# First loads, unit sizes, casts and last group of an attention-then-MoE kernel rearranged on one Trainium2 core

## The chip, the cores and the metric

The kernel runs on 1 core of one Trainium2 (trn2) chip. The metric is device microseconds of one execution. Before the change the median of 4 runs is 959.17 us (958.56 to 964.36).

## The reference, cut to what matters

Attention with pooled keys feeds a two-layer MLP. All inputs and the output are float32.

```python
# B, C, Hh, Ww = 4, 128, 384, 32 ; r = 4 ; d_ff = 2048
kv_pool = kv.reshape(B, H//r, r, W//r, r, C).mean(axis=(2, 4))
kv_flat = kv_pool.reshape(B, -1, C) @ w_sr          # 768 keys per batch, k = v
s = scale * (q @ k.transpose(0, 2, 1))
a = np.exp(s - s.max(-1)); a /= a.sum(-1) + 1e-09
x = a @ v                                           # 49152 tokens x 128
h = x @ w_in                                        # 128 -> 2048
out = (h * (1 / (1 + np.exp(-1.702 * h)))) @ w_out  # 2048 -> 128
```

## The kernel before

**Tiling.** The 49152 tokens are cut into 96 groups of 512 (`NG`), four groups make a set (`s`, 24 of them), 24 groups are one batch. A batch has 768 keys in 6 chunks of 128 (`JC`). The MLP's 2048 hidden columns are 16 chunks of 128 (`FCH`). The work goes attention of groups 0 to 47, MLP of groups 0 to 47, attention of 48 to 95, MLP of 48 to 95. The attention of a few chunks (the four groups 48 to 51, and eight "rolling" chunks) has its exponential on VectorE instead of ScalarE.

**Units.** TensorE fills one half of PSUM banks 0 to 5 with up to three chunks of 128x512 scores (`fill_attn`, L335 to 340) or hidden values (`fill_moe`, L517 to 521); one ScalarE instruction evicts the unit as Exp or Gelu into `ag`. Units go alternately to banks 0 to 2 and 3 to 5, and unit p's fill waits for ScalarE's end of unit p-2. Later TensorE *drains* what was evicted: attention weights times V into bank 6 or 7 (`drain_attn`, L349), or w_out times the activations into bank 6 or 7 (`drain_moe`, L526). The list `sizes` (L542) gives the chunks of the first units: two of 1, seven of 2, then (3, 3, 2) four times; all others have 3. The first attention part has 286 chunks, so its last unit holds 1 chunk.

**Order.** The program is written out in order by hand. `first` (L600) names what TensorE does ahead of the first 21 units: pooling of key chunks (`pool_chunk`, L136), keys and values (L145, L150, L158, L159), transposes of q (`transpose_q`, L229) and dummy matmuls (`warm`, L286). `prepare` calls `background(i)` (L456) when group i is first met, and a loop with estimated costs (`COST`) places the drains and extras. Each engine runs its own instructions in this order.

**Loads.** At the start group 0 and group 1 of q come as float32 on SyncE's and ScalarE's queues into `ag` (L240), are cast by ScalarE (L258), transposed by TensorE (L229) and evicted by ScalarE (L233); groups 2 to 15 come by casting DMAs from GpSimd's queue (`load_q`, L218) and their transposes are evicted by VectorE (L235). The key chunks of batch 0 come in the same GpSimd queue (`load_chunk`, L127), the first two in halves. From set 4 on, q is cast in HBM to `q_bf` by GpSimd's queue (`cast_q`, L206) and loaded by a transposing DMA from SyncE's queue (`load_qT`, L211) into one of four `qT` buffers. In `background`, at every fourth group, set s+3 is loaded so and set s+5 is cast; `gate` (L447) is a one-element memset on VectorE followed by one on GpSimd over the same element, so that GpSimd's next DMA goes out only when VectorE has come to that place. At groups 10 and 13 three key chunks each of batch 1 are loaded.

**End.** A group's output gathers over 16 chunks as 128 output columns by 512 tokens in one bank, is transposed in 32x32 blocks by VectorE (L534) and leaves in four DMAs of 64 KB (L537), whose contiguous pieces are 32 floats, 128 bytes. For the last group two of them go by SyncE's queue and two by ScalarE's.

Of the kernel before, what the change touches and what calls it, by code (L numbers as in the profile page):

```python
# [7 lines left out]
F32 = mybir.dt.float32  # L8
F32R = mybir.dt.float32r
I32 = mybir.dt.int32  # L10
BF = mybir.dt.bfloat16
# [13 lines left out]
def kernel(  # L25
    ctx, tc, q, kv, w_sr, moe_w_in, moe_w_out, out,
):
    nc = tc.nc
# [7 lines left out]
    FCH = d_ff // 128  # L36
    scale = 1.0 / (C ** 0.5)
    G = 512
# [5 lines left out]
    K = 3  # L44
# [76 lines left out]
    def load_chunk(b, jc, n=1):  # L121

        a, ch = divmod(jc, HC)
        t = x_tile(XS - 1 - jc)
        for k in range(n):
            sl = slice(k * SG // n, (k + 1) * SG // n)
            nc.gpsimd.dma_start(out=t[:, sl], in_=kv_r[b, a, ch][:, sl])  # L127
        kv_tiles[b, jc] = t.rearrange("p (wp w1 c) -> p w1 wp c", w1=r, c=C)
# [75 lines left out]
    def cast_q(s):  # L204
        sl = slice(s * SG, (s + 1) * SG)
        nc.gpsimd.dma_start(out=q_bf[sl, :].rearrange("(p i) c -> p (i c)", p=128),  # L206
                            in_=q_flat[sl, :].rearrange("(p i) c -> p (i c)", p=128))

    def load_qT(s):
        qTs[s] = qpool.tile([128, 1, SG], BF, name="qT")  # L210
        nc.sync.dma_start_transpose(out=qTs[s], in_=q_bf[s * SG:(s + 1) * SG, :])  # L211


# [8 lines left out]
    def transpose_q(g):  # L222
        s = g // 4
        if g % 4 == 0:
            qTs[s] = qpool.tile([128, 1, SG], BF, name="qT")
        ps = acc_bf()[:, 0:G].rearrange("p (i t) -> p i t", i=4)
        for i in range(4):
            o = (g % 4) * G + i * 128
            nc.tensor.transpose(ps[:, i, :], qs[s][:, o:o + 128], ident)  # L229
        dst = qTs[s][:, 0, (g % 4) * G:(g % 4 + 1) * G].rearrange("p (t i) -> p t i", i=4)  # L230
        src = ps.rearrange("p i t -> p t i")
        if g < 2:
            nc.scalar.copy(dst, src)  # L233
        else:
            nc.vector.tensor_copy(dst, src)  # L235

    ag = agpool.tile([128, AG, 512], BF, name="ag")
    raw = ag[:, 0:4, :].bitcast(F32)
    for g, eng in ((0, nc.sync), (1, nc.scalar)):
        eng.dma_start(out=raw[:, 2 * g:2 * g + 2, :],  # L240
                      in_=q_flat[g * G:(g + 1) * G, :].rearrange("(p k i) c -> p k (i c)", p=128, k=2))
    w_sr_f = cpool.tile([128, C], F32)
    nc.sync.dma_start(out=w_sr_f, in_=w_sr)
    load_chunk(0, 0, 2)
    load_chunk(0, 1, 2)
    load_q(0, 2, 4)
    load_q(1, 0, 2)
# [6 lines left out]
    load_q(3, 0, 2)  # L254
    load_q(3, 2, 4)
    cast_q(4)
    for g in range(2):
        nc.scalar.copy(qs[0][:, g * G:(g + 1) * G].rearrange("p (k e) -> p k e", k=2), raw[:, 2 * g:2 * g + 2, :])  # L258

    ones = cpool.tile([128, 32], BF)  # L260
    nc.vector.memset(ones, 1.0)
# [21 lines left out]
    def warm(n):  # L283

        for _ in range(n):
            nc.tensor.matmul(banks[:32, 2, :], ones, ones.unsqueeze(1).broadcast_to([128, 16, 32]),  # L286
                             start=True, stop=True)
# [1 line left out]
    w_in_sb = cpool.tile([128, d_ff], BF)  # L289
    w_out_sb = cpool.tile([128, FCH, C], BF)  # L290

    warm(7)
    transpose_q(0)
    transpose_q(1)
    warm(4)


    slot_of = {}
# [148 lines left out]
    def gate():  # L447

        one = gate_tile[:, gates[0] % 8:gates[0] % 8 + 1]
        gates[0] += 1  # L450
        nc.vector.memset(one, 0.0)  # L451
        nc.gpsimd.memset(one, 0.0)  # L452

    CAST = 5

    def background(i):  # L456

        s = i // 4
        if i % 4 == 0:
            if QS <= s + 3 < NS:  # L460
                load_qT(s + 3)
            if CAST <= s + CAST < NS:
                gate()
                cast_q(s + CAST)
        if i in (10, 13):
            gate()
            for jc in range(i - 10, i - 7):
                load_chunk(1, jc)
        if 0 <= i - 16 < JC:
            extras.append((key_and_value, 1, i - 16))  # L470
        if 0 <= i - 15 < JC:
            extras.append((pool_chunk, 1, i - 15))
        if i in (30, 34, 38):
            put_away(0, (i - 30) // 4)
        if i in (33, 37, 41):
            bring_back(0, (i - 33) // 4)
        if i == 26:
            gate()
            nc.gpsimd.dma_start(out=w_in_sb, in_=moe_w_in)
        if i == 34:  # L480
            gate()
            nc.gpsimd.dma_start(out=w_out_sb, in_=moe_w_out.rearrange("(o p) c -> p o c", p=128))
# [40 lines left out]
    def drain_moe(g, fc):  # L523
        if fc == 0:
            o_of[g] = acc(("o", g))
        nc.tensor.matmul(o_of[g], w_out_sb[:, fc, :], weights(("m", g, fc)),  # L526
                         start=(fc == 0), stop=(fc == FCH - 1))
        del slot_of["m", g, fc]
        if fc == FCH - 1:
            close(("o", g), max(now, dve - 1.0) + EVACUATE)  # L530
            on_dve(3.6)

            o_sb = opool.tile([128, 512], F32, name="o_sb")
            nc.vector.transpose(o_sb, o_of.pop(g))  # L534
            for m in range(4):
                eng = nc.scalar if g == NG - 1 and m % 2 else nc.sync
                eng.dma_start(out=out_r[g, m],  # L537
                              in_=o_sb[32 * m:32 * m + 32, :].rearrange("i (b j) -> i b j", j=32))


    NA, NM = NG * JC, NG * FCH
    chunks, sizes = [], [1] * 2 + [2] * 7 + [3, 3, 2] * 4  # L542
    chunks += [(0, 0), (1, 0), (0, 1), (1, 1)]
    chunks += [(i, jc) for i in range(2, 8) for jc in range(2)]
    chunks += [(i, jc) for jc in range(2, JC) for i in range(8)]
# [3 lines left out]
    for n in range(R):  # L549
        part = [c for c in chunks if c[0] // (NG // R) == n]  # L550
        while part:
            m = sizes.pop(0) if sizes else K
            seq.append(("a", part[:m]))
            part = part[m:]
        todo += [("a", t, a) for t in range(n * NT // R, (n + 1) * NT // R) for a in range(2)
                 if (t // TS * TS + TS - 1) // 4 not in early]
        flat = [(g, fc) for g in range(n * NG // R, (n + 1) * NG // R) for fc in range(FCH)]
        todo += [("m",) + c for c in flat]
        for k in range(0, len(flat), K):
            seq.append(("m", flat[k:k + K]))  # L560

    at = {}
    for p, (kind, part) in enumerate(seq):
# [15 lines left out]
    def prepare(p):  # L579
# [18 lines left out]
                free[last_acc] = now + COST[f][1]  # L598

    first = {  # L600
        0: [(pool_chunk, 0, 0), (warm, 1), (key_chunk, 0, 0), (warm, 1)],
        2: [(value_chunk, 0, 0), (warm, 1), (pool_chunk, 0, 1), (warm, 1), (key_and_value, 0, 1), (warm, 1)],
        3: [(transpose_q, 2), (transpose_q, 3)],
        4: [(transpose_q, 4)],
        5: [(transpose_q, 5)],
        6: [(transpose_q, 6)],
# [141 lines left out]
```

## Time and profile before

| | |
|---|---|
| median of 4 runs | 959.17 us |
| the profiled execution, its time | 958.56 us |
| its span in the profile | 956.5 us |
| ScalarE (ACT) busy | 941.4 us, 98% |
| TensorE matmul (PE) busy | 942.7 us, 99% |
| VectorE (DVE) busy | 382.4 us, 40% |
| GpSimd (POOL) busy | 68.8 us, 7% |
| mean DMA rate | 99 GB/s |

The profile's page lists busy time by engine, the span in slices, the DMA queues, the chain of work that ended last, the costliest groups of instructions and the DMA issues. A matmul's duration in it overlaps that of the next one, so a busy PE is not a PE at its limit; the same is true of ScalarE, where an activation's record can begin while the one before still runs. The distance between the starts of two successive instructions is then the better measure. "L340" is line 340 of the kernel shown above. Times in the timeline are microseconds from the start of the span.

### The profile page before, as it was taken

How to read it: one execution, taken by the hardware profiler on the slowest of the kernel's cores; microseconds unless marked ns; L12 is line 12 of the kernel's file. 1: busy time of each engine (PE TensorE's matmuls, PEld its weight loads, DVE VectorE, ACT ScalarE, POOL GpSimd, SP SyncE). 2: the span in 40 equal slices, each digit the busy share in tenths (PEclk: the TensorE clock that was granted, in tenths of full speed). 3: DMA queues.
4: the chain of work that ended last, by engine and by line, in shares of the span. 5: the costliest groups of instructions: out<-in, count | busy, mean ns of one | idle time of the engine just before them, and what ended most of it. 6: DMA issues, size and time to landing. Idle time of an engine off the chain costs nothing.

```text
span 956.5 us, 15155 instructions
## 1 busy us (share of the span) xinstructions
PE 942.7 (99%) x6280; PEld 501.8 (52%) x6280; DVE 382.4 (40%) x801; ACT 941.4 (98%) x707; POOL 68.8 (7%) x118
## 2 busy tenths in 40 slices
PE   7899999999999999999999999999999999999997
PEld 3677777444444444454446777754444444444443
DVE  4443553111578778777645774320110101101010
ACT  6999999999999999999999999999999999999997
POOL 4110101330000332000000000000000000000000
PEclk9999999999999999999999999999999999999999
DMA  9997991999852798215268964562222222222222
GB/s 197 214 202 127 206 195 38 150 139 177 165 110 39 113 147 107 43 27 84 34 102 151 177 148 96 123 126 40 45 33 45 39 40 44 35 45 37 41 35 43
DMA packets 373092, 94.64 MB, mean 99 GB/s; under 512 B 346720, under 2 KB 370144, under 8 KB 372704
## 3 DMA queue, kind: packets, MB, share of 16 engines
q1 hardware_dynamic: 342656, 61.04, 36.5%
q0 software_dynamic: 29168, 32.25, 22.2%
q8 instruction: 49, 0.80, 0.3%
q10 hardware_dynamic: 1200, 0.39, 0.2%
q14 instruction: 19, 0.16, 0.1%
HBM read 52.49 MB, written 48.23 MB: 105 GB/s over the span
## 4 chain that ended last, share of the span: by engine, by line
ACT 96%; PE 1%; issue 1%; DMA 1%; DVE 0%; POOL 0%; DVEq 0%; ACTq 0%; POOLq 0%
ACT ag L521 72%; ACT ag L340 24%; PE banks L338 1%; DMA x<-in_kv_dram 1%; ACT L521 0%; DVE qT L235 0%; PE banks L229 0%; PE banks L136 0%; ACT L340 0%; PE banks L349 0%; PE banks L526 0%; PE banks L519 0%; DVE o_sb L534 0%; POOL x L127 0%; DVE kT L160 0%
## 5 line engine op out<-in xcount | busy, mean ns | idle before, releaser
L521 ACT ACTIVATE ag<-banks 128x1536 bf16<-128x1536 f32 x512 | 688.3, 1523 | 0.0
L519 PE MATMUL banks<-x,w_in_sb 128*128 128x512 bf16 x1536 | 414.9, 379 | 0.3 <-ACT ag L340 0.3
L526 PE MATMUL banks<-ag,w_out_sb 128*128 128x512 bf16 x1536 | 412.3, 379 | 0.5 <-ACT ag L521 0.5
L340 ACT ACTIVATE ag<-banks 128x1536 bf16<-128x1536 f32 (+2 forms) x187 | 245.7, 1480 | 5.5 <-PE banks L338 5.3
L526 PEld LDWEIGHTS <-w_out_sb 128*128 128x128 bf16 x1536 | 150.0, 98 | 180.6 <-issue 1.2
L519 PEld LDWEIGHTS <-w_in_sb 128*128 128x128 bf16 x1536 | 148.2, 98 | 171.6 <-issue 6.0
L534 DVE STREAM_TRANSPOSE o_sb<-banks 128x512 f32<-128x512 f32 x96 | 68.7, 716 | 378.4 <-PE banks L526 365.7
L349 PEld LDWEIGHTS <-ag 128*128 128x128 bf16 x2272 | 145.5, 98 | 43.7 <-issue 0.5
L349 PE MATMUL banks<-v,ag 128*128 128x129 bf16 x2272 | 162.9, 220 | 0.1
L338 PE MATMUL banks<-qT,kT 128*128 128x512 bf16 x544 | 147.6, 379 | 4.9 <-ACT ag L340 3.5
L408 DVE SCALAR_TENSOR_TENSOR ea<-ea,eb 128x512 f32<-128x512 f32 x128 | 88.0, 687 | 3.4
L363 DVE TENSOR_TENSOR x<-banks,rec 128x384 bf16<-128x384 f32 x128 | 71.3, 557 | 4.4
L360 DVE RECIPROCAL rec<-banks 128x3 f32<-128x3 f32 x128 | 22.9, 179 | 104.4 <-PE banks L349 104.0
L338 PEld LDWEIGHTS <-kT 128*128 128x128 bf16 x544 | 47.0, 98 | 32.6 <-issue 4.6
L170 POOL DMA_DIRECT2D kvs<-in_kv_dram x32 | 40.6, 1318 | 28.8 <-DMA kvs<-in_kv_dram 26.6
L397 DVE TENSOR_SCALAR ea<-banks 128x512 f32<-128x512 f32 x32 | 22.1, 692 | 39.6 <-PE banks L381 39.6
L452 POOL MEMSET gate_tile<- 1x1 f32 x39 | 4.6, 117 | 431.0 <-DVE gate_tile L451 430.9
L403 DVE SCALAR_TENSOR_TENSOR eb<-eb,ea 128x512 f32<-128x512 f32 x32 | 21.9, 686 | 0.7
L410 DVE SCALAR_TENSOR_TENSOR ag<-ea,ee 128x512 bf16<-128x512 f32 x24 | 16.5, 688 | 0.9
L405 DVE TENSOR_SCALAR ea<-eb 128x512 f32<-128x512 f32 x32 | 14.2, 445 | 0.9
L401 DVE TENSOR_SCALAR ee<-eb 128x512 int32<-128x512 f32 x32 | 13.5, 423 | 0.9
L399 DVE TENSOR_SCALAR eb<-ea 128x512 f32<-128x512 f32 x32 | 13.5, 422 | 0.8
(62 smaller groups left out, 144.3 us busy)
## 6 DMA issues: line engine op xcount, KB each, us to landing
out_dram<-o_sb SPq DMA_DIRECT2D x382, 64.0 KB, 2.0
x_bf<-x SPq DMA_DIRECT2D x16, 768.0 KB, 6.4
kvs<-in_kv_dram POOLq DMA_DIRECT2D x32, 384.0 KB, 6.4
q_bf<-in_q_dram POOLq DMA_DIRECT2D x20, 512.0 KB, 7.6
x<-in_kv_dram POOLq DMA_DIRECT2D x10, 512.0 KB, 10.9
x<-in_q_dram POOLq DMA_DIRECT2D x7, 256.0 KB, 13.9
x<-in_kv_dram POOLq DMA_DIRECT2D x4, 256.0 KB, 6.1
w_in_sb<-in_moe_w_in_dram POOLq DMA_DIRECT2D x1, 512.0 KB, 5.1
```

The source lines that it names most:

```text
L170: nc.gpsimd.dma_start(out=kv_sums[b][:, i2], in_=kv_p[b, i, w, :, i2], **({"accum_op": ADD} if n else {}))
L338: nc.tensor.matmul(ps[:, k, :], kTs[i // GB][:, jc * 128:(jc + 1) * 128], rhs, start=True, stop=True)
L340: nc.scalar.activation(place([("a",) + c for c in chunks]), ps, AF.Exp, scale=scale)
L349: nc.tensor.matmul(av_of[u][:, k * (C + 1):(k + 1) * (C + 1)], weights(("a", i, jc))[:, o:o + T], vs[i // GB][:, jc, 0:C + 1], start=(jc = ...
L360: nc.vector.reciprocal(rec, ps[:, :, C])
L363: nc.vector.tensor_tensor(to, ps[:, :, 0:C], rec.unsqueeze(2).broadcast_to([128, TS, C]), MUL)
L397: nc.vector.tensor_scalar(a, ps, scale / LN2, -126.0, MUL, MAX)
L408: nc.vector.scalar_tensor_tensor(a, a, COEFFS[k], b, ADD, MUL)
L519: nc.tensor.matmul(ps[:, k, :], w_in_sb[:, fc * 128:(fc + 1) * 128], x[:, g % (4 * XS) * G:(g % (4 * XS) + 1) * G], start=True, stop=True)
L521: nc.scalar.activation(place([("m",) + c for c in chunks]), ps, AF.Gelu_apprx_sigmoid)
L526: nc.tensor.matmul(o_of[g], w_out_sb[:, fc, :], weights(("m", g, fc)), start=(fc == 0), stop=(fc == FCH - 1))
L534: nc.vector.transpose(o_sb, o_of.pop(g))
```

## The change

Six things are changed.

1. The two float32 loads of q with ScalarE's casts go. Groups 0 and 1 of q are loaded by casting DMAs of one group each on GpSimd's queue, between key chunk 0 and key chunk 1. Group 1's transpose is evicted by VectorE. The dummy matmuls and q transposes at the start are placed anew.
2. The unit sizes of the first attention part become two of 1, eight of 2, (3, 3), then (3, 3, 2) twice, and 3 from there, so that its last unit has 3 chunks.
3. In the first round, sets 4 to 14 are loaded at the groups in `TURN` and sets 5 to 16 cast at those in `CAST`, instead of every fourth group; the second three key chunks of batch 1 are loaded at group 12 instead of 13.
4. Each transposing load is preceded by a VectorE memset of one column of its buffer, so the load waits for VectorE to reach that place.
5. The last 18 MLP chunks are evicted in eight units of 2 and two of 1, instead of six of 3.
6. The last group's output is gathered with the activations as the stationary operand: four 128x128 matmuls a chunk instead of one of 128x512, into banks 2, 5, 6 and 7, so that tokens are rows. One of the four, whose bank is still held by the group before, is begun three chunks late. VectorE evicts two blocks, ScalarE the other two, and each half leaves in one DMA of 128 KB with contiguous pieces of 512 bytes.

```diff
     def load_qT(s):
         qTs[s] = qpool.tile([128, 1, SG], BF, name="qT")
+        nc.vector.memset(qTs[s][:, 0, 0:1], 0.0)
         nc.sync.dma_start_transpose(out=qTs[s], in_=q_bf[s * SG:(s + 1) * SG, :])
...
-        if g < 2:
+        if g == 0:
             nc.scalar.copy(dst, src)
...
-    ag = agpool.tile([128, AG, 512], BF, name="ag")
-    raw = ag[:, 0:4, :].bitcast(F32)
-    for g, eng in ((0, nc.sync), (1, nc.scalar)):
-        eng.dma_start(out=raw[:, 2 * g:2 * g + 2, :],
-                      in_=q_flat[g * G:(g + 1) * G, :].rearrange("(p k i) c -> p k (i c)", p=128, k=2))
     w_sr_f = cpool.tile([128, C], F32)
     nc.sync.dma_start(out=w_sr_f, in_=w_sr)
     load_chunk(0, 0, 2)
+    load_q(0, 0, 1)
+    load_q(0, 1, 2)
     load_chunk(0, 1, 2)
...
-    for g in range(2):
-        nc.scalar.copy(qs[0][:, g * G:(g + 1) * G].rearrange("p (k e) -> p k e", k=2), raw[:, 2 * g:2 * g + 2, :])
...
-    warm(7)
-    transpose_q(0)
-    transpose_q(1)
-    warm(4)
+    ag = agpool.tile([128, AG, 512], BF, name="ag")
+    warm(13)
...
-    CAST = 5
+    TURN = {4: 4, 8: 5, 18: 6, 21: 7, 24: 8, 27: 9, 29: 10, 32: 11, 36: 12, 40: 13, 44: 14}
+    CAST = {0: 5, 4: 6, 13: 7, 19: 8, 22: 9, 25: 10, 28: 11, 32: 12, 36: 13, 40: 14, 44: 15, 46: 16}
...
-        s = i // 4
-        if i % 4 == 0:
-            if QS <= s + 3 < NS:
-                load_qT(s + 3)
-            if CAST <= s + CAST < NS:
-                gate()
-                cast_q(s + CAST)
-        if i in (10, 13):
+        first_round = i < GB * 2
+        s = TURN.get(i, NS) if first_round else i // 4 + 3 if i % 4 == 0 else NS
+        if s < NS:
+            load_qT(s)
+        s = CAST.get(i, NS) if first_round else i // 4 + 5 if i % 4 == 0 else NS
+        if s < NS:
             gate()
-            for jc in range(i - 10, i - 7):
+            cast_q(s)
+        if i in (10, 12):
+            gate()
+            for jc in range(i % 10 * 3 // 2, i % 10 * 3 // 2 + 3):
                 load_chunk(1, jc)
...
+        if g == NG - 1:
+            drain_last(g, fc)
+            return
...
+    def drain_last(g, fc):
+
+        own = (2, 5, 6, 7)
+        held = own.index(13 - last_acc)
+        parts = [(m, fc) for m in range(4) if m != held or fc > 2]
+        if fc == 2:
+            parts += [(held, f) for f in range(3)]
+        for m, f in parts:
+            nc.tensor.matmul(banks[:, own[m], 0:T], weights(("m", g, f))[:, m * T:(m + 1) * T], w_out_sb[:, f, :],
+                             start=(f == 0), stop=(f == FCH - 1))
...
+        if fc == FCH - 1:
+            o_sb = opool.tile([128, 512], F32, name="o_sb").rearrange("p (k c) -> p k c", k=4)
+            nc.vector.tensor_copy(o_sb[:, 0:2, :], banks[:, 2:6:3, 0:T])
+            nc.scalar.copy(o_sb[:, 2:4, :], banks[:, 6:8, 0:T])
+            for m, eng in ((0, nc.sync), (2, nc.scalar)):
+                lo = g * G + m * T
+                eng.dma_start(out=out[lo:lo + 2 * T, :].rearrange("(k p) c -> p k c", p=T), in_=o_sb[:, m:m + 2, :])
...
-    chunks, sizes = [], [1] * 2 + [2] * 7 + [3, 3, 2] * 4
+    chunks, sizes = [], [1] * 2 + [2] * 8 + [3, 3] + [3, 3, 2] * 2
...
-        for k in range(0, len(flat), K):
-            seq.append(("m", flat[k:k + K]))
+        rest = [2] * 8 + [1, 1] if n == R - 1 else []
+        while flat:
+            m = K if len(flat) > sum(rest) else rest.pop(0)
+            seq.append(("m", flat[:m]))
+            flat = flat[m:]
...
-        0: [(pool_chunk, 0, 0), (warm, 1), (key_chunk, 0, 0), (warm, 1)],
-        2: [(value_chunk, 0, 0), (warm, 1), (pool_chunk, 0, 1), (warm, 1), (key_and_value, 0, 1), (warm, 1)],
-        3: [(transpose_q, 2), (transpose_q, 3)],
+        0: [(pool_chunk, 0, 0), (transpose_q, 0), (warm, 1), (key_chunk, 0, 0), (transpose_q, 1)],
+        1: [(value_chunk, 0, 0), (warm, 1)],
+        2: [(pool_chunk, 0, 1), (warm, 2), (key_and_value, 0, 1), (warm, 1), (transpose_q, 2)],
+        3: [(transpose_q, 3)],
```

More of the change, by code (lines that the diff above doesn't have):

```diff
@@ L535, in drain_moe @@
             for m in range(4):
-                eng = nc.scalar if g == NG - 1 and m % 2 else nc.sync
-                eng.dma_start(out=out_r[g, m],
-                              in_=o_sb[32 * m:32 * m + 32, :].rearrange("i (b j) -> i b j", j=32))
+                nc.sync.dma_start(out=out_r[g, m],
+                                  in_=o_sb[32 * m:32 * m + 32, :].rearrange("i (b j) -> i b j", j=32))
+    def drain_last(g, fc):
[7 more added lines that the diff above has]
+                             start=(f == 0), stop=(f == FCH - 1))
+        if fc == 2:
+            for f in range(2):
+                del slot_of["m", g, f]
+        if fc > 1:
+            del slot_of["m", g, fc]
+        if fc == FCH - 1:
[5 more added lines that the diff above has]
+                eng.dma_start(out=out[lo:lo + 2 * T, :].rearrange("(k p) c -> p k c", p=T), in_=o_sb[:, m:m + 2, :])
     NA, NM = NG * JC, NG * FCH
-    chunks, sizes = [], [1] * 2 + [2] * 7 + [3, 3, 2] * 4
+    chunks, sizes = [], [1] * 2 + [2] * 8 + [3, 3] + [3, 3, 2] * 2
     chunks += [(0, 0), (1, 0), (0, 1), (1, 1)]
```

## The prediction

> **What bounds the kernel now.** I read the page's engine shares first, then the costliest groups, then what ScalarE (ACT) waited for.
>
> ```profile
> PE 942.7 (99%) x6280; PEld 501.8 (52%) x6280; DVE 382.4 (40%) x801; ACT 941.4 (98%) x707; POOL 68.8 (7%) x118
> ...
> ACT 96%; PE 1%; issue 1%; DMA 1%; DVE 0%; POOL 0%; DVEq 0%; ACTq 0%; POOLq 0%
> ```
>
> ```profile
> ACT ag L340 <- PE banks L338: 5.3, 4, 2.9
> ACT x L258 <- DMA ag<-in_q_dram: 2.0, 1, 2.0
> ACT L258 <- PEq L732: 1.2, 1, 1.2
> ACT L521 <- PE banks L519: 0.4, 1, 0.4
> ```
>
> The reader sees a ScalarE that is 96% of the chain that ended last and in 956.5 us waits for little: 5.3 us for score matmuls, nearly all before 20 us, and 0.4 us where Gelu begins. No load makes it wait after 20 us. TensorE (PE) is close behind: starts of MLP units are 1.343 us apart, in which it does six 512-column matmuls 215 ns apart, 1.29 us. So time can be won only at the start, in the number and joints of units, and after the last activation. Those places are in the timeline; first the start.
>
> ```profile
> 1.27 2.29 POOL L127 DMA_DIRECT2D x<-in_kv_dram  x4 [0.81 <-POOLq L732]
> ...
> 7.75 0.37 PE L136 MATMUL banks<-sum,x 128*128 128x32 bf16 x8 [0.38 <-DMA x<-in_kv_dram]
> ...
> 9.62 1.08 ACT L340 ACTIVATE ag<-banks 128x512 bf16<-128x512 f32 x2 [2.88 <-PE banks L338]
> ...
> 12.35 1.02 ACT L340 ACTIVATE ag<-banks 128x1024 bf16<-128x1024 f32 x1 [1.65 <-PE banks L338]
> ...
> 13.96 5.60 ACT L340 ACTIVATE ag<-banks 128x1024 bf16<-128x1024 f32 x6 [0.59 <-PE banks L338]
> ```
>
> Key chunk 0 is asked for at 1.27 and used at 7.75; the first exponential starts at 9.62, the third unit only at 12.35. Then the end.
>
> ```profile
> 948.81 1.79 ACT L521 ACTIVATE ag<-banks 128x1536 bf16<-128x1536 f32 x1
> ...
> 950.65 0.81 PE L526 MATMUL banks<-ag,w_out_sb 128*128 128x512 bf16 x3 [0.54 <-ACT ag L521]
> ...
> 951.49 0.72 DVE L534 STREAM_TRANSPOSE o_sb<-banks 128x512 f32<-128x512 f32 x1 [5.57 <-PE banks L526]
> 952.24 0.85 SPq L537 DMA_DIRECT2D out_dram<-o_sb  x2
> 952.24 0.93 ACTq L537 DMA_DIRECT2D out_dram<-o_sb  x2
> ```
>
> From ScalarE's end (950.60) to the span's end pass 5.9 us: three matmuls, a transpose of 0.72, four output DMAs. The last lands at 955.46, 3.22 after the first issue.
>
> **1. First loads.** In the DMA records the two float32 loads move from 1.79 to 4.36, and GpSimd's first packet comes at 4.06, 2.79 after its issue. Where its queue was idle, later ones came after 1.26 (w_in, issued 83.80), 1.54 and 1.88 (key sums, 156.41 and 316.12). I read that the float32 loads held it back by about 1.2 and take the first packet at S = 2.85 (1.27 + 1.58); bounds 2.5 and, if nothing is won, 4.06. Everything follows S at the old pace: chunk 0 landed 3.64 after its first packet (7.70), so now at 6.5. A q group costs a casting queue 0.69 (172 ns for a packet that reads 4 KB, 64 such reads' worth on 16 engines), so group 0 lands at 7.2, group 1 at 7.9, and all behind them shift by 2 x 0.69 - 1.21 = +0.17: chunk 1 at 10.35 (10.19), q groups 2 and 3 at 11.7 (11.51), chunk 5 at 25.8 (25.66). TensorE now has group 1's transposes ahead of the first scores: 7.9, plus four transposes to about 8.3, scores, exponential near 8.8 to 8.9. But unit 2 waits for chunk 1 and has group 2's transposes ahead of it: 11.7 + 0.4, then 0.6 of scores, so about 12.6, 0.25 later. Group 3's transposes no longer stand with group 2's, so unit 3 starts near 13.75 instead of 13.96. What reaches the steady part is **-0.2** (bounds -0.55 and +1.0). ScalarE's two casts and one copy are gone; they were early anyway. VectorE's new copy (0.69) lies before unit 1, which is early as well.
>
> The Trainium skill, "DMA: Bandwidth & Descriptors", Latency and other measured facts, gives about 0.6 us to the first byte for a load queued by SyncE or ScalarE and about 1 us for GpSimd's. This speaks against moving the loads; the trace had 1.04 and 2.79. By the page alone S would be 2.3 and the start 0.5 better, an estimate.
>
> **2. Unit sizes.** A unit of 2 that follows a unit of 2 takes 0.90, one that follows a 3 takes 1.01. One unit and two such joints fewer, and three more chunks in plain threes: 44 chunks from unit 3 on took 20.54 us (13.96 to 34.50); as 7 x 0.905 + 2.69 + 2 x 3.69 + 8 chunks at 0.449 they take 20.0. **-0.5.** What could cap it is chunk 5: landed 25.66, pooled from 26.71, 1.05 of slack, of which this eats 0.7 and the later landing 0.15. Bounds -0.7 and 0.
>
> **3. A full last attention unit.** Its single-chunk unit starts at 141.64 and Gelu's table load at 142.70: 1.06, where a single takes 0.48, so 0.58 lost. After the two full units before a table load 0.29 and 0.14 are lost. **-0.4** (bounds -0.6 and 0).
>
> **4. TURN, CAST and the memset.** The gates show when VectorE reaches a group: 33.9 (8), 45.6 (12), 56.3 (16), 66.5 (20), 77.9 (24), 87.5 (28), 99.5 (32). Set 6, asked for at group 18, goes out near 61.4; ScalarE starts group 24 near 77.9 (34.5 plus 96 chunks at 0.452) and its fill runs some 2.4 earlier, so it is needed at 75.5; set 7, at 21, near 69 for 86; sets 8 to 11 have 19 us and more. The median transposing load lands 9.0 after issue in the first 150 us. SyncE's queue behind a waiting load holds the x store of group 30 and what follows, needed only from 142 on. A memset of one column takes some 60 ns on a VectorE half idle there; behind it wait evictions that TensorE needs, but it waits only for a buffer whose last reader is at or before the fill just being issued. GpSimd's casts go out later with 9.9 us or more to the load (99.5 to 109.4, groups 32 to 36), and land in 7.8 at the median. Nothing is won either, since ScalarE waited for no load here: **0**, covered by 14 us for set 6; without cover, see the second rival.
>
> **5 and 6. The end.** The last 18 chunks as threes are 6 x 1.343 = 8.06; as eight twos and two ones 8 x 0.905 + 2 x 0.477 = 8.19. TensorE needs, for a two, 2 x 215 + 8 x 56 (the spacing of the attention drains at L349, the same form) = 0.88, just below 0.905; I use 0.92, so ScalarE ends at 950.9. But behind its last fill, at 949.9, TensorE has 24 of the new matmuls: 0.22 + 24 x 0.056 + 0.22 of latency, done at 951.7, **+0.2** against 951.49. Evicting 128x256: copies of 128x128 and 128x512 from PSUM take 0.29 and 0.69, so 0.42 on VectorE beside 0.39 on ScalarE, **-0.3**. The DMAs: 2048 packets of 128 bytes took 12.5 to 13.8 ns each on 16 engines, 1.7; 512 packets of 512 bytes take 27 ns (w_sr's load), 0.86; and each queue's second issue, 0.36 to 0.42 later, goes. With 0.84 to the first packet and 0.40 after the last, 2.1 instead of 3.22: **-1.1**. The end wins 1.2 (bounds 0.3, with the two evictions one after the other and slower stores, and 1.8).
>
> The Trainium skill, "TensorE: Matmul & The Clock Gate", Back-to-back issue gap, gives 81 ns sustained for 128 columns and 131 for 512. This speaks against step 6. Here the rows say 56 and 215; by the page the 24 matmuls would take 0.6 more and the end would win 0.6, an estimate.
>
> **Sum**, against the profiled execution's own 958.56 (span 956.5 and 2.06 around it): -0.2 - 0.5 - 0.4 + 0 - 1.2 = -2.3, so 956.3. The median of the runs shown is 959.17, 0.6 higher, and I forecast such a median: **956.9**. Both ends of the bounds give 955.5 and 959.9.
>
> **Rivals.** *The queue isn't freed*: S stays 4.06 since GpSimd's first issue is itself slow (0.69 where others take 0.55), and every load is 1.38 late instead of 0.17. For it: no software packet lies among the float32 ones. Against: the three idle cases. +1.2, so 958.1.
>
> *A transposing load comes late, slower than before.* In the trace set 6's load went out at 44.24 and landed at 67.81, 23.6 later, among key loads. Now its request waits for VectorE until 61.4. It decides from a latency of 14 us; at 23.6 ScalarE stands for 9.5: 966.4. For it: that row. Against: the key loads of batch 1 are then over (57 or earlier), and all other such loads before 150 us took 13.2 or less.
>
> *The joints close*: attention units of 3 start 1.356 apart where 1.330 is the floor, 2.1 over 79 units; if the new order of drains frees TensorE there, 954.8. Against: nothing removed lies in TensorE's way there.
>
> **Chances.** Forecast 0.70 (955.5 to 958.0), queue not freed 0.13, late load 0.07, joints 0.07, the rest between. Range 954.6 to 960.3, which leaves out the late load and the ends. A measurement tells about 0.5% from no change, 4.8 us: faster 0.05 (the joints with a better end), within 0.88, slower 0.07 (the late load).
>
> **What would show it.** First GpSimd packet near 2.85 and first exponential near 8.8; a unit at or before 13.8 and then no longer wait; about 0.3 between the last Exp and the table load; set 6 landed before 75; last landing about 2.1 after its issue. Wrong would be score matmuls that wait for `qT`, chunk 1 landing after 11, or 24 last matmuls wider than 56 ns apart.

## The result, and the profile after

The changed kernel has a median of 957.54 us (956.90 to 959.53, 53 runs); the kernel before, beside it, 959.10 us. The medians differ by 1.56 us. The ratio of the two, which goes by means, is 0.9978, with a 95% interval of 0.9970 to 0.9985: 2.1 us of 959. Both are less than the 0.5% that the prediction calls no difference. The profiled execution took 957.27 us with a span of 955.5 (before: 958.56 and 956.5). Ratios here leave out executions more than 1.5% above the fastest of their kernel; of before's 79 executions 18 are above 961 us, and those of them up to 969 still count in the ratio and hardly in the median. Without all 18 the means differ by 1.35 us.

The same views as before the change, after it. First the engines' busy time and the chain that ended last.

```profile
PE 944.4 (99%) x6330; PEld 504.4 (53%) x6330; DVE 383.1 (40%) x822; ACT 940.2 (98%) x708; POOL 68.9 (7%) x120
...
ACT 86%; PE 12%; DMA 1%; issue 0%; DVE 0%; POOL 0%; POOLq 0%
```

ScalarE (ACT) has 1.2 us less to do, TensorE (PE) 1.7 more. The chain's share of ACT fell from 96% to 86%, yet the middle of the kernel is not a microsecond different (the ledger below): where two engines are equally tight, the chain may be followed back through either. A share of the chain is not a time to be won.

What ScalarE waited for, in us (total, times, longest):

```profile
ACT qT L234 <- PE banks L230: 6.4, 1, 6.4
ACT ag L334 <- PE banks L332: 3.6, 4, 2.2
ACT L234 <- PEq L757: 0.8, 1, 0.8
ACT o_sb L556 <- PE banks L546: 0.7, 1, 0.7
```

Two rows are gone: the wait at Gelu's first unit (0.4 before), and the one for a load (2.0 before). The 6.4 us is idle time that the removed casts used to fill; it cost nothing by itself. The start, in the timeline of all engines (start, duration, engine, line, operation):

```profile
1.27 1.23 POOL L127 DMA_DIRECT2D x<-in_kv_dram  x2 [0.81 <-POOLq L757]
...
6.63 0.84 PE L136 MATMUL banks<-sum,x 128*128 128x32 bf16 x16
...
8.03 0.40 PE L230 MATMUL banks<-ident,x 128*128 128x128 bf16 x4 [0.56 <-DMA x<-in_q_dram]
```

and in that of ScalarE alone:

```profile
9.74 0.60 ACT L334 ACTIVATE ag<-banks 128x512 bf16<-128x512 f32 x1 [0.69 <-PE banks L332]
10.76 0.60 ACT L334 ACTIVATE ag<-banks 128x512 bf16<-128x512 f32 x1 [0.42 <-PE banks L332]
13.56 8.91 ACT L334 ACTIVATE ag<-banks 128x1024 bf16<-128x1024 f32 x9 [2.21 <-PE banks L332]
```

The first exponential starts at 9.74, not near 8.8; unit 2 at 13.56, not near 12.6. But units 2, 3 and the next seven now run as one group with no wait between them, where before unit 3 waited 0.59 more. The table load (ScalarE) and the end (all engines):

```profile
136.80 5.64 ACT L334 ACTIVATE ag<-banks 128x1536 bf16<-128x1536 f32 x4
142.46 1.28 ACT L517 ACT_TABLE_LOAD   x1
```

```profile
949.96 1.50 PE L546 MATMUL banks<-w_out_sb,ag 128*128 128x128 bf16 x24
951.44 0.42 DVE L555 COPY o_sb<-banks 128x256 f32<-128x256 f32 x1 [5.63 <-PE banks L546]
951.50 0.37 ACT L556 COPY o_sb<-banks 128x256 f32<-128x256 f32 x1 [0.74 <-PE banks L546]
951.89 0.40 SPq L559 DMA_DIRECT2D out_dram<-o_sb  x1
951.90 0.47 ACTq L559 DMA_DIRECT2D out_dram<-o_sb  x1
```

Nothing stands between the last Exp and the table load. The two evictions start at 951.44 and 951.50 and take 0.42 and 0.37, where the old transpose started at 951.49 and took 0.72. The last landing is at 954.21, 2.32 after the first issue.

**A ledger by stage** shows it in one table. Unit 3 is chosen as a mark because it begins with chunk 4 in both kernels; the 41st chunk begins a unit in both.

| stage, us | before | after | difference | forecast |
|---|---|---|---|---|
| to the start of unit 3 | 13.96 | 14.52 | +0.56 | -0.2 |
| to the 41st chunk | 16.86 | 16.56 | -0.30 | -0.45 |
| to the first Gelu table load | 111.88 | 111.38 | -0.50 | -0.5 |
| to the last 18 MLP chunks | 799.39 | 799.45 | +0.06 | 0 |
| to the last landing | 13.37 | 12.30 | -1.07 | -1.2 |
| to the end of the span | 1.04 | 1.29 | +0.25 | 0 |

The forecast's terms 2 and 3 (-0.5 and -0.4) are cut at the 41st chunk here: by their own numbers the stretch before it should have taken 7 x 0.905 + 2.69 + 2 x 3.69 = 16.40, and the 8 chunks behind it 0.10 less. The six differences add up to the span's -1.0. Each is one execution against one; the experiments say which of them hold. The second and third rows, those of the sizes, repeat: they are 16.56 to 16.58 and 111.38 to 111.40 in all eight kernels with the new sizes and no late load, 16.85 to 16.86 and 111.88 to 111.90 in the three with the old ones. The last row went between 1.04 and 1.30 in the kernels profiled, with no order that I can explain.

### The profile page after: what moved, and what is told of

The parts are those of the page before. It is cut to its first block, busy times and chain, and to the rows that moved or that the text cites. A ratio compares the mean times of both kernels' runs of the same rounds, so it can differ in the third digit from the quotient of the medians.

```text
span 955.5 us, 15292 instructions
## 1 busy us (share of the span) xinstructions
PE 944.4 (99%) x6330; PEld 504.4 (53%) x6330; DVE 383.1 (40%) x822; ACT 940.2 (98%) x708; POOL 68.9 (7%) x120
## 4 chain that ended last, share of the span: by engine, by line
ACT 86%; PE 12%; DMA 1%; issue 0%; DVE 0%; POOL 0%; POOLq 0%
ACT ag L517 72%; ACT ag L334 14%; PE banks L343 6%; PE banks L332 5%; DMA x<-in_kv_dram 1%; PE banks L136 0%; POOL x L127 0%; DVE x L357 0%; PE banks L230 0%; PE banks L546 0%; ACT L517 0%; ACT L334 0%; POOL x L219 0%; PE banks L515 0%; PE banks L282 0%
## 5 line engine op out<-in xcount | busy, mean ns | idle before, releaser
L517 ACT ACTIVATE ag<-banks 128x1536 bf16<-128x1536 f32 (+1 forms) x516 | 688.7, 1513 | 0.0
L399 DVE TENSOR_SCALAR ea<-eb 128x512 f32<-128x512 f32 x32 | 13.9, 434 | 0.8
```

The costliest lines, as they stand in the source:

```text
L517: nc.scalar.activation(place([("m",) + c for c in chunks]), ps, AF.Gelu_apprx_sigmoid)
```

## The experiments

The theory: in the middle of the kernel nothing can be won, and the gain is that of three small terms: the unit sizes, the full last unit, and the end; the new groups of the loads cost and win nothing; the start is the doubtful term. The rivals are named with each.

### The start: loads against order

**e1** has the changed kernel's end, sizes and groups with the whole old start (its edit also gives the eviction of group 1's transposes back to ScalarE).

```diff
+    raw = ag[:, 0:4, :].bitcast(F32)
+    for g, eng in ((0, nc.sync), (1, nc.scalar)):
+        eng.dma_start(out=raw[:, 2 * g:2 * g + 2, :],
+                      in_=q_flat[g * G:(g + 1) * G, :].rearrange("(p k i) c -> p k (i c)", p=128, k=2))
...
-    load_q(0, 0, 1)
-    load_q(0, 1, 2)
...
+    for g in range(2):
+        nc.scalar.copy(qs[0][:, g * G:(g + 1) * G].rearrange("p (k e) -> p k e", k=2), raw[:, 2 * g:2 * g + 2, :])
...
-    warm(13)
+    warm(7)
+    transpose_q(0)
+    transpose_q(1)
+    warm(4)
...
+        0: [(pool_chunk, 0, 0), (warm, 1), (key_chunk, 0, 0), (warm, 1)],
+        2: [(value_chunk, 0, 0), (warm, 1), (pool_chunk, 0, 1), (warm, 1), (key_and_value, 0, 1), (warm, 1)],
+        3: [(transpose_q, 2), (transpose_q, 3)],
```

> The changed kernel with the whole start of before: float32 loads of groups 0 and 1 on SyncE's and ScalarE's queues, ScalarE's casts, the old order of TensorE's first work. Theory (first traffic 0.87 us later): key chunk 1 lands near 10.2 instead of 11.28, chunk 5 near 25.7 instead of 26.42, unit 3 starts near 13.9 instead of 14.52 and Gelu's first table load comes 0.4 to 0.8 earlier than 142.46; about 0.6 us faster than the changed kernel. Rival (the order of TensorE): the same here, since the order goes back too; it differs in the next two runs.

**e2** puts back the loads and casts alone, the diff of e1 down to the line with `nc.scalar.copy`; `warm(13)` and `first` stay as changed, and with them TensorE's order.

```diff
-    load_q(0, 0, 1)
-    load_q(0, 1, 2)
...
+    for g in range(2):
+        nc.scalar.copy(qs[0][:, g * G:(g + 1) * G].rearrange("p (k e) -> p k e", k=2), raw[:, 2 * g:2 * g + 2, :])
```

> The changed kernel with only the loads of before (float32, ScalarE's casts), TensorE's order as changed. Theory: loads as before (chunk 1 near 10.2, q groups 2 and 3 near 11.5), so unit 2 starts near 12.5 and unit 3 near 13.4 to 13.9; 0.6 us or more faster than the changed kernel. Rival (the new order of transposes ahead of the first scores costs the time): unit 3 stays near 14.5 though the loads are early, no gain.

**e3** keeps the new loads, and puts group 1's transposes behind the first scores and group 2's beside group 3's.

```diff
-        0: [(pool_chunk, 0, 0), (transpose_q, 0), (warm, 1), (key_chunk, 0, 0), (transpose_q, 1)],
-        1: [(value_chunk, 0, 0), (warm, 1)],
-        2: [(pool_chunk, 0, 1), (warm, 2), (key_and_value, 0, 1), (warm, 1), (transpose_q, 2)],
-        3: [(transpose_q, 3)],
+        0: [(pool_chunk, 0, 0), (transpose_q, 0), (warm, 1), (key_chunk, 0, 0)],
+        1: [(value_chunk, 0, 0), (transpose_q, 1), (warm, 1)],
+        2: [(pool_chunk, 0, 1), (warm, 2), (key_and_value, 0, 1), (warm, 1)],
+        3: [(transpose_q, 2), (transpose_q, 3)],
```

> The changed kernel with its new loads, but group 1's transposes placed behind the first scores and group 2's behind unit 2's scores. Theory: unit 0 starts some 0.3 earlier than 9.74, but unit 3 still waits for q groups 2 and 3, which land at 12.64, so it stays at 14.3 to 14.6 and the time does not change by 0.2 us. Rival (order): unit 3 goes back to about 13.9 and the kernel is 0.6 us faster.

Measured: e1 957.31 us, ratio 0.9973 (0.9953 to 0.9992); e2 956.59, 0.9966 (0.9945 to 0.9988); e3 957.85, 0.9984 (0.9963 to 1.0004). The three intervals overlap each other's and the changed kernel's, so by times alone no order of the four is settled. Not all came as expected: unit 3 starts at 14.66 in e1 (13.9 expected) and at 15.06 in e3 (14.3 to 14.6), and at 14.00 in e2, near what was expected. The profiles separate the parts. ScalarE's timeline in e1:

```profile
13.05 1.02 ACT L341 ACTIVATE ag<-banks 128x1024 bf16<-128x1024 f32 x1 [1.65 <-PE banks L159]
14.66 7.95 ACT L341 ACTIVATE ag<-banks 128x1024 bf16<-128x1024 f32 x8 [0.59 <-PE banks L339]
```

and in e2:

```profile
13.04 10.25 ACT L338 ACTIVATE ag<-banks 128x1024 bf16<-128x1024 f32 x10 [1.63 <-PE banks L230]
```

Unit 2 starts at the same time in both. In e1 unit 3 comes 1.61 later, in e2 0.96, with no wait. This 1.61 is the same in every kernel with the old order, before among them, and in e3, which has the old order at this place with the new loads (its first exponential starts at 9.46, 0.28 earlier than in the changed kernel, and its unit 3 at 15.06, 0.54 later). With the new order it is 0.96 or 0.97 in all eight kernels that have it. So **the order of the transposes wins 0.65 us** between these two units, whatever the loads.

The loads lose about as much. Key chunk 1, for which unit 2 waits, lands at 10.34 on average over the seven kernels with float32 loads (9.89 to 10.78) and at 11.15 over the seven without (10.70 to 11.71). Two queues shared the first microseconds before; now GpSimd's alone does. The DMA lines of the first 12 us, of before:

```profile
DMA packets 1525, 2.14 MB, mean 179 GB/s; under 512 B 135, under 2 KB 757, under 8 KB 1525
```

and after:

```profile
DMA packets 1334, 1.70 MB, mean 142 GB/s; under 512 B 123, under 2 KB 822, under 8 KB 1334
```

By these lines 0.44 MB less has been moved by then (1.70 against 2.14). Of this, 0.26 is a matter of counting: groups 0 and 1 of q are 256 packets of 2 KB in before, where they arrive as float32, and 256 of 1 KB after, where a casting DMA is recorded with the bf16 that it writes. The other 0.18 MB is late.

Putting both together, unit 3 starts at a median of 14.65 over five kernels with the old start (13.96, 14.59, 14.65, 14.66, 14.82) and of 14.33 over the six with the new one (13.94, 14.07, 14.15, 14.52, 14.62, 15.41); the means are 14.54 and 14.45. This difference is less than the scatter, and the executions don't bear it out: the medians' 1.56 is less than the 1.87 that the sizes and the end win in the ledger, and e1 with the old start is no slower than the changed kernel. **Whether the new start wins or costs a few tenths is not shown.**

Why before's 13.96 is so early, the granted clock of TensorE tells. In the old start TensorE has seven dummy matmuls and then waits 1.02 to 1.19 us, from 4.14 on, for the float32 loads and their casts. The full clock was granted from 4.7 in before, but from 8.7, 9.4, 9.8 and 10.0 in the other four kernels with this start. In e10, whose start is the same code as before's, the four dummy matmuls behind the first transposes took 1.89 us instead of 1.04, and unit 2 started 0.69 later though key chunk 1 had landed 0.30 earlier. In the nine kernels with thirteen dummy matmuls in a row the full clock came between 4.2 and 6.8. The ledger's +0.56 compares with an early start of before.

### The sizes and the groups of the loads

**e10** is the kernel before with `TURN`, `CAST`, the 12 and the memset; nothing else.

```diff
+        nc.vector.memset(qTs[s][:, 0, 0:1], 0.0)
...
-            if QS <= s + 3 < NS:
-                load_qT(s + 3)
-            if CAST <= s + CAST < NS:
...
+        s = TURN.get(i, NS) if first_round else i // 4 + 3 if i % 4 == 0 else NS
...
+        s = CAST.get(i, NS) if first_round else i // 4 + 5 if i % 4 == 0 else NS
...
-        if i in (10, 13):
+        if i in (10, 12):
```

> The kernel before with TURN, CAST, the key loads at groups 10 and 12 and the memset, and nothing else. Theory: the median stays at 959.1 within 0.4 us (nothing is won in an undisturbed execution), but none of some ten executions lies above 961, where the kernel before has 18 of 79 above it, up to 991. Rival (the schedule wins or costs in every execution): a median 0.5 us or more away.

958.96 us, ratio 0.9996 (0.9988 to 1.0005), none of its 11 executions above 961 us: the 0 of step 4, for this kernel. **e6** is the kernel before with only the sizes of the attention units new.

```diff
-    chunks, sizes = [], [1] * 2 + [2] * 7 + [3, 3, 2] * 4
+    chunks, sizes = [], [1] * 2 + [2] * 8 + [3, 3] + [3, 3, 2] * 2
```

> The kernel before with only the new unit sizes of the first attention part. Theory: the fortieth chunk is reached 0.3 to 0.5 us earlier, and 0.45 us are won where the last full unit hands over to Gelu's table load (0.13 lost instead of 0.58); 0.7 to 1.0 us below before in all. Rival (the wins of the sizes are given back by TensorE, which is as busy): 0.3 us or less.

It should have won 0.9 by the forecast's terms 2 and 3, and in its trace the stretch from unit 3 to the 41st chunk does take the new 16.56. It took 980.62 us at the median (958.60 to 1006.53, 12 runs), ratio 1.0039 (1.0002 to 1.0076); 10 of its 12 executions were above 961. What TensorE waited for in it:

```profile
PE banks L136 <- DMA x<-in_kv_dram: 22.9, 2, 22.1
```

A key load of batch 1, asked for at 40.7 and landed at 75.4, stopped TensorE for 22 us. **e4** is the converse: the changed kernel with the old groups and no memset.

```diff
-        nc.vector.memset(qTs[s][:, 0, 0:1], 0.0)
...
-        s = TURN.get(i, NS) if first_round else i // 4 + 3 if i % 4 == 0 else NS
...
-        s = CAST.get(i, NS) if first_round else i // 4 + 5 if i % 4 == 0 else NS
...
+            if QS <= s + 3 < NS:
+                load_qT(s + 3)
+            if CAST <= s + CAST < NS:
...
-        if i in (10, 12):
+        if i in (10, 13):
```

> The changed kernel with the old schedule of casts and transposing loads at every fourth group, key chunks of batch 1 at groups 10 and 13, and no memset ahead of the loads. Prediction's step 4 (nothing won or lost): the stage from the fortieth chunk to Gelu's table load as long as in the changed kernel within 0.3 us, and set 6's load slow again, near 20 us, without a wait of ScalarE for it. Rival (the new schedule removes stalls of TensorE or ScalarE in attention): 0.5 to 2 us slower than the changed kernel.

967.62 us (960.85 to 981.80, 12 runs), ratio 1.0068 (1.0036 to 1.0099). In the profiled execution score matmuls waited 4.8 us for `qT` of set 5, asked for at 40.2 and landed at 70.2. My expectation failed: the groups are not neutral once the sizes are new. Two parts of step 4 could be the one that matters, so each was taken back by itself: **e9** drops the memset and keeps the groups, which is the first line of e4's diff:

```diff
-        nc.vector.memset(qTs[s][:, 0, 0:1], 0.0)
```

**e11** keeps the memset and takes the old groups, the rest of that diff:

```diff
-        s = TURN.get(i, NS) if first_round else i // 4 + 3 if i % 4 == 0 else NS
...
-        if i in (10, 12):
+        if i in (10, 13):
```

> The changed kernel without the memset ahead of the transposing loads; TURN and CAST stay. Theory (a transposing load under way while GpSimd's key loads of batch 1 arrive slows both): SyncE runs ahead to the next load as soon as a buffer and its cast are ready, so set 6 goes out near 42 instead of 60.4, in the middle of the key loads (40 to 59), takes 20 us and more, and single executions lie 3 to 40 us above 957.5, unevenly. Rival (it is the groups at which loads and casts stand that matter, the memset is idle): median within 0.4 us of 957.5 and no execution above 960.

> The changed kernel with the memset kept, but loads, casts and key loads at the old groups. Theory: set 6's load now waits for VectorE at group 12, about 45, which is still among the key loads, so it lands 20 us later and executions scatter above 960 as without the memset. Rival (the memset alone keeps the loads apart): median within 0.4 us of 957.5, none above 960.

e9: 957.89 us (957.04 to 958.47), ratio 0.9985 (0.9977 to 0.9994), as the changed kernel. Without the memset set 6's load did go out early, at 44.3, and took 21.5 us among the key loads, but it is needed only at 75. e11: 971.27 us (957.56 to 989.33, 12 runs), ratio 1.0045 (1.0014 to 1.0075); in the profile TensorE waits 16.4 us for `qT`, and it is that of set 5, not of set 6 as I expected. My theory for e9 fell and its rival held: **the groups matter and the memset does not**.

What happens with the old groups is seen in the DMA queues from 33 to 60 us (packets, MB, share of sixteen engines' time; q0 is GpSimd's queue, in q1 most packets are the transposing loads' 256 bytes). In before, in an execution with no late load:

```profile
q0 software_dynamic: 888, 4.30, 80.2%
q1 hardware_dynamic: 4669, 1.18, 25.5%
```

In e6:

```profile
q0 software_dynamic: 459, 2.67, 60.7%
q1 hardware_dynamic: 2500, 0.63, 57.5%
```

After:

```profile
q0 software_dynamic: 938, 4.19, 78.8%
q1 hardware_dynamic: 4160, 1.05, 21.5%
```

A share times 16 engines times 27 us, divided by the packets, gives a packet's mean time in q1: 24 ns in before, 22 after, and 99 in e6, where both queues together move 40% less in the same time (3.30 MB against 5.48). Few packets make this mean: the median is 18 ns in all three, but in e6 113 of the 2468 packets of 256 bytes took more than 0.5 us, and these hold 71% of the queue's time (23 of 4605 in before, 10 of 4096 after). e11 looks like e6 (mean 77 ns); in e4, where set 5's load is late too, the mean is only 29. The engines also fall out of step: a load is finished when the last of its sixteen parts has landed. In before the parts of the first key load of batch 1 land between 45.4 and 46.0; in e6 thirteen of them between 50.4 and 54.4, and three at 75.4.

Which load suffers is read from issues and landings. A transposing load that is in flight among the key loads takes long in every trace: set 6's 23.6 us in before (44.2 to 67.8) and 21.5 in e9, where nobody needs it yet; set 5's 30 us in e4 (40.2 to 70.2), 42 in e6 (37.7 to 79.6) and 52 in e11 (39.0 to 90.6), where TensorE needs it near 65. In the changed kernel set 5's load goes out at 37.8 and is down at 42.2, as the key loads begin. The old groups put the cast of set 7 (group 8) at 33 to 34 us, beside set 4's load and ahead of set 5's; in e6 and e11 both it and set 4's load take 18 to 22 us, so that set 5's load is still behind them when the key loads come. In e4 these two are on time and only set 5's is late. The new groups put that cast at group 13, behind the key loads (47.8 in the changed kernel).

The executions say the same. Of the 36 of e4, e6 and e11, 31 took more than 961 us; of the 53 of the changed kernel and the 88 of the other kernels with the new groups none took more than 959.9. The kernel before itself took more than 961 us, up to 991, in 33 of 184 executions (18 of the 79 beside the changed kernel, 15 of the 105 beside the experiments). None of those is among the profiled ones; that late loads made them long is inferred from the kernels with the same groups.

### The end

**e5** is the kernel before with the new end (steps 5 and 6) alone, **e7** the changed kernel with the small units but the old drain of the last group, **e8** the changed kernel with four stores of 64 KB, two by each queue, instead of two.

```diff
+        if g == NG - 1:
+            drain_last(g, fc)
+            return
...
-        for k in range(0, len(flat), K):
-            seq.append(("m", flat[k:k + K]))
+        rest = [2] * 8 + [1, 1] if n == R - 1 else []
```

The first of these is e5's (with `drain_last` itself). That of e7, and that of e8:

```diff
-        if g == NG - 1:
-            drain_last(g, fc)
-            return
```

```diff
-            for m, eng in ((0, nc.sync), (2, nc.scalar)):
+            for m, eng in ((0, nc.sync), (2, nc.scalar), (1, nc.sync), (3, nc.scalar)):
                 lo = g * G + m * T
-                eng.dma_start(out=out[lo:lo + 2 * T, :].rearrange("(k p) c -> p k c", p=T), in_=o_sb[:, m:m + 2, :])
+                eng.dma_start(out=out[lo:lo + T, :].rearrange("(k p) c -> p k c", p=T), in_=o_sb[:, m:m + 1, :])
```

> The kernel before with the new end alone (eight units of 2 and two of 1, the last group's tokens as rows, two stores). Theory (most of the gain is the end): the last landing 1.0 to 1.2 us earlier than in the kernel before, relative to the same start of the last 18 chunks; the time 0.9 to 1.3 us below before. Rival (the end wins little, the gain is in the joints): under 0.4 us.

> The changed kernel with the small last units but the old drain of the last group (one 512-column matmul a chunk, block transpose, four stores). It tells the small units from the stores by rows. Theory: ScalarE ends 0.1 to 0.3 us later than with units of 3, the last matmuls end a little earlier than with 3 (one chunk instead of three behind the last activation, 0.4 us less), so about as long an end as before; 1.0 us slower than the changed kernel. Rival (small units are where the end wins): at most 0.4 us slower than the changed kernel.

> The changed kernel with four stores of 64 KB in pieces of 512 bytes, two on each queue, instead of two of 128 KB. Theory (packet size, and one issue a queue): the second issue comes 0.36 to 0.42 after the first, so the last landing comes 0.3 to 0.4 us later than 2.32 after the first issue, and still 0.5 earlier than the 3.22 of before. Rival (all of the win is packet size): the landing stays within 0.1 of 2.32.

Measured: e5 958.28 us (0.9983; 0.9965 to 1.0002), e7 958.44 (0.9987; 0.9970 to 1.0004), e8 957.04 (0.9975; 0.9958 to 0.9992). From the first of the last 18 chunks to the last landing the traces give 13.36 or 13.37 in the three kernels with the old end (before, e6, e10), 12.26 to 12.38 in the ten with the new one, and 13.47 in e7. So **there is no gain without the row drain**; the small units without it lose 0.1. The end of e7's timeline says why they don't help:

```profile
949.52 1.46 PE L522 MATMUL banks<-ag,w_out_sb 128*128 128x512 bf16 x6
951.01 0.72 DVE L530 STREAM_TRANSPOSE o_sb<-banks 128x512 f32<-128x512 f32 x1 [5.65 <-PE banks L522]
951.75 0.85 SPq L533 DMA_DIRECT2D out_dram<-o_sb  x2
```

ScalarE's last activation ends 8.84 us behind the first of the last 18 chunks, where before it was 8.50, and six matmuls are left for TensorE behind its last fill. The row drain with units of 3 was not run, so what the small units add beside it is open. By the timelines of before and after, the 1.07 is made of +0.13 until the last eviction starts, -0.30 for the eviction and -0.90 from the first issue to the last landing. And within the row drain, the count of stores is nothing: e8 issues two to a queue like the kernel before and lands 2.35 after its first issue, against 2.32. The DMA lines from 950 us to 957 us show what does it. In before:

```profile
q10 hardware_dynamic: 1056, 0.13, 13.0%
q1 hardware_dynamic: 1056, 0.13, 12.4%
```

and in e8:

```profile
q10 hardware_dynamic: 288, 0.13, 6.3%
q1 hardware_dynamic: 288, 0.13, 6.2%
```

The same bytes in pieces of 512 instead of 128 take half of the engines' time: 25.4% of 7 us is 1.78, 12.5% is 0.88.

### A version that might beat both

**e12** joins what looked best: e2 with e8's four stores (both diffs above).

> The changed kernel with the float32 first loads of before and TensorE's order as changed, and the last group stored in four DMAs instead of two: the best version that the runs point to. Theory: first traffic at 1.8, third exponential unit near 13.0, so 0.9 us below the changed kernel as when the loads alone went back (956.59), and four stores change it by less than 0.3; 956.2 to 956.7. Rival (the 0.9 was an accident of that chip): 957.2 or more.

957.19 us (956.28 to 959.90), ratio 0.9978 (0.9968 to 0.9987): not better than the changed kernel, and 0.6 above e2 though their difference should be nothing (the two ran on different chips). Its profiled execution, of 957.29, shows what differed. The columns are the stretch, its length, busy time and instructions of PE, PEld, DVE, ACT and POOL, the granted clock, the DMA share and GB/s:

```profile
5.20:8.60 3.40, 1.77 (x25) 0.98 (x23) 0.42 (x3) 0.41 (x2) 2.02 (x4) 1.00 1.09 177
8.60:12.00 3.40, 3.39 (x27) 1.49 (x27) 1.39 (x7) 1.71 (x3) 1.38 (x3) 0.50 1.19 203
```

TensorE's clock was halved from 8.6 to 12.0, and the same stretch in e2 has 1.00. Unit 3 started at 14.78 here and at 14.00 in e2. No version is shown to beat the changed kernel; the old loads with the new order are the candidate, by 0.95 us of medians in e2 and 0.35 in e12, with overlapping intervals.

## Why the prediction was right, point by point

The forecast median was 956.9 and the measured one is 957.54. The forecast's -2.3 is -1.6 by the medians. The sizes and the end make -1.87 by their rows, which leaves about +0.3 for the start and all else, where -0.2 was forecast. The -2.1 of the ratio is nearer, but it counts executions of before between 961 and 969 us, to which the forecast gave nothing: that nearness is luck. The terms for the sizes and the end are right in mechanism; the chain of the start is not.

- **What bounds it**: right. Between the table load and the last 18 chunks 799 us changed by 0.06. The third rival, joints that close, did not come, though the order of drains changed.
- **The start** (-0.2; not settled). GpSimd's first packet was forecast at 2.85 and came at 2.66 (before 4.06), so the queue was freed and the first rival falls. The step that failed is the next one, "Everything follows S at the old pace": chunk 0 landed 4.40 after the first packet (7.06) instead of 3.64, groups 0 and 1 took 0.93 and 0.82 instead of 0.69, and chunk 1, which was to land 0.17 later, lands 0.8 later on average. The changed kernel's first packets are slow: 417, 277 and 190 ns on average in the three half microseconds from 2.5 on, against the 172 of the forecast's row. In the seven kernels with float32 loads it is the first packets of those that are slow, 278 to 794 ns on average from 1.5 to 2.0 against 84 from 3.0 on, and GpSimd's first ones behind them take 172 or 173. So I read, without an experiment on it alone, that the float32 loads took the slow time upon themselves.

  What offset it was the piece of the forecast I valued least: "Group 3's transposes no longer stand with group 2's", 0.65. Unit 3, forecast at 13.75, came at 13.94 to 15.41. The forecast also took the profiled 13.96 of before for the rule, where the other four old starts, whose full clock came late, have 14.59 to 14.82.

  The Trainium skill, "DMA: Bandwidth & Descriptors", Latency and other measured facts, puts GpSimd's first byte at about 1 us; here it came 1.39 after its issue (1.27 to 2.66) when nothing held the queue. The measurement decides.
- **Unit sizes and the full last unit** (-0.9; -0.80). Right in mechanism. The term "7 x 0.905" was 0.16 too small: from 14.52 to 21.02 these seven units took 6.50, since one of them (at 19.06, the same one in e1 and e2) took 1.03. The joint at the table load gave the forecast's 0.4 and a little: the last Exp starts 1.46 ahead of it, of which 1.33 is a full unit's own, so 0.13 is lost instead of 0.58.
- **Step 4** (0). The number holds where it was given, e10. The argument does not: I looked for cover for the loads in the new order and found 14 us, and did not ask what cover the old order had. By e4, e6 and e11 the old groups were one step from loads that take 30 to 52 us. The second rival (a transposing load comes late, 966.4) exists, but it stands on the side of the old groups. That e4's 967.62 is near its price is chance: the price was 9.5 us of waiting for set 6, and e4's trace has 4.8 for set 5. With the new groups set 6's load, out at 60.4, landed at 64.3, eleven before it was needed.
- **The end** (-1.2; -1.07). Right, piece by piece: +0.2, -0.3 and -1.1 were forecast for the last matmuls, the evictions and the stores, and +0.13, -0.30 and -0.90 came. The row drain's 24 matmuls went 56 ns apart (1.50 less one of 0.21 over 23); the 81 ns that the prediction sets against this do not hold here. Of the reasons given for the stores, the size of the pieces is the whole and the second issue nothing (e8).

## What stays open

Which single move of the new groups suffices was not tried: the cast of set 7 is what the traces point to, but the second key loads and the later casts moved with it. Nor is it known why the new sizes make late loads more frequent (2 of 12 executions are above 961 in e5, 10 of 12 in e6), nor what on the DMA engines makes some of the 256-byte packets take over 0.5 us once it begins, nor why in e4 loads are late with few such packets. The order e2, after, e3 is argued from the traces and not settled by times, and so is the sign of the new start as a whole. Why the full clock comes late in most old starts is not known either; thirteen dummy matmuls in a row were tried with the old loads (e2, e12), but not with the old order.

## What to carry to other kernels

Judge the cover of a load by many executions or by undoing the schedule, not by one profile: a profile in which no load is late says only that none was late that time. Before taking work off a second queue at the start, look at what it takes upon itself: in all fourteen traces the first 2 KB packets were slow, whichever queue they came by. Before comparing two starts by one profile each, look at when TensorE's full clock was granted. For the last store choose long contiguous pieces first; the number of DMAs matters less.

## What the runs showed of the hardware that I had not expected

- **DMA engines can fall out of step.** With casting DMAs and transposing loads at once, 113 of 2468 packets of 256 bytes on the hardware queue took more than 0.5 us in e6, 1.5 us on average, while the median stayed at 18 ns; three of the sixteen parts of a load landed 21 us after the others.
- **The clock of TensorE can fall to half for 3.4 us while it has work.** In e12 the clock was full from 5.2, TensorE waited for key chunk 0 from 6.3 to 7.95, so that it was busy 1.77 us of the 3.40 up to 8.6 (the fence above), and then had 0.50 of the clock until 12.0. In e11 it was full from 6.15, TensorE was busy 2.19 of the 3.41 up to 9.56 with no wait above 0.8, and then had 0.50 until 13.0. With the same start as e12, e2 kept the full clock, though of the first 3.41 us behind 4.24, when it was granted, TensorE was busy only 1.67. So busy time alone does not tell when it falls. The Trainium skill, "TensorE: Matmul & The Clock Gate", What's actually happening, tells of a free-running window of 3413 ns, which the 3.4 us stretches agree with, and of a gate that closes after at least one idle window; here it closed after windows half or more of which were busy, and the measurement decides.
